# One tile per pair for the local exponentials, a mask added in three steps, and a new order of the plan

## The chip, the cores and the metric

The kernel runs on one core of a Trainium2 chip. The metric is the device time of one execution in microseconds (us). Before the change it is 983.41 us, the median of three runs (981.79 to 986.02). For this kernel about 0.5%, 4.9 us, can be told from no change.

The core has five engines with an instruction stream each: PE (TensorE, matmuls; PEld is its weight loads), DVE (VectorE), ACT (ScalarE), POOL (GpSimd) and SP (SyncE, which here only issues DMAs). They wait for each other and for DMAs through semaphores.

## The reference

Two attentions over q, k, v of shape 8 x 8 x 576 x 64 are added, and a feed-forward layer with a rational activation follows:

```python
q_d, k_d, v_d = (x.reshape(B, H, S // 4, 4, D).mean(axis=3) for x in (q, k, v))
out_up = np.repeat(sm_attn(q_d, k_d, v_d), 4, axis=2)        # attention among means of 4 tokens
mask = np.abs(pos[:, None] - pos[None, :]) < 4
scores = np.where(mask, scale * q @ k.T, -1e9)               # local attention, 7 tokens wide
out_local = softmax(scores) @ v
x = (out_up + out_local).transpose(0, 2, 1, 3).reshape(4608, 512)
h = x @ w_in                                                 # 512 -> 2048
P = a[0] + a[1] * h + a[2] * h**2 + a[3] * h**3
Q = 1 + abs(b[0]) * abs(h) + abs(b[1]) * h**2
out = (P / (Q + 1e-6)) @ w_out                               # 2048 -> 512
```

## The kernel before

**The layer.** The 4608 tokens are cut into blocks: eight of 512 tokens (one per batch) and a last one of the 64 tokens left of each batch. A block of 512 has 16 steps. In a step PE makes a 128 x 512 piece of h (line 1087, 12 matmuls), ACT and DVE make the activation from it (`middle`; ACT line 1100, DVE lines 1144 to 1193, each over 128 x 512), and PE multiplies the two parts of the result, `g`, into the output sums (line 1217, 12 matmuls). Line 1179 writes `g`; the first matmul of line 1217 waits for it.

**The attention.** Two heads make a pair, two pairs a quad, so a block has two quads. While PE works on the layer of one block, the attention of a later block is worked in between. From block 3 on (`begin`, called for ten quads, called far quads below) a quad goes like this. SP loads q and k. PE makes the local scores: 10 windows of 58 queries against 64 keys for each pair, two windows of one column of 64 to each head (line 484). DVE adds the mask while it moves the scores from PSUM to SBUF (line 498), takes the maximum (592), scales it (619); ACT takes the exponentials in place, 10 instructions a pair (627); DVE divides by the sums (668, 669, 692). These numbers then have to be turned. DVE turns 32 x 32 blocks (779, into `tt`), and SP sends them through DRAM to put the blocks in their places: four writes `bounce<-tt` and two reads `eu<-bounce` a pair (747). The pooled attention takes the same way (754, 757, `bounce_p`, `eq`). PE then multiplies with the values (929, 891).

**Where the tiles lie.** The scores, the exponentials (`el`) and what comes back from DRAM (`eu`) of a pair share one place in SBUF. The places of the two pairs of a quad (slots 0 and 1) lie side by side, and a tensor `els` is laid over both. All instructions on `el` of either pair go through views of `els` (lines 310 to 312), which lets one mask addition cover the last column of the first pair and all five columns of the second (line 519). `eu0` and `eu1` are tensors of their own at the same addresses (line 301).

**What sets the order.** Each piece of work is recorded as a task with the engine, an assumed duration, and the 32-byte pieces of SBUF or banks of PSUM that it reads and writes (`add`; `part` gives a view its own pieces). `Plan.run` then walks through time and puts the tasks of each engine in an order by their latest start; a table `SHIFT` moves that latest start, task by task. The instructions are issued in that order. It is the plan's own bookkeeping, by pieces, that decides the order; the semaphore waits are put in afterwards by the framework, by the tensors that instructions use.

```python
both = put("els", [P, NW, 2, D], F32, slots[0].el.at)
s.el = part(both, both.ap[:, i * NW // 2 : (i + 1) * NW // 2], i * n, n)
self.eu = put(f"eu{i}", [P, 4, NW // 2, BL], F32, self.el.at)
```

Of the kernel before, what the change touches and what calls it, by code (L numbers as in the profile page):

```python
# [20 lines left out]
P = 128  # L21
# [50 lines left out]
class Task:  # L72
    __slots__ = ("engine", "dur", "fn", "due", "preds", "succs", "late", "start", "end", "n", "load", "at", "key", "wait", "land", "big")


class Plan:
# [16 lines left out]
    def add(self, engine, dur, fn, reads=(), writes=(), due=None, load=None, at=0.0, wait=2.05, big=False):  # L93
# [3 lines left out]
        t.key, t.wait, t.big = self.key, wait, big  # L97
# [27 lines left out]
    def run(self):  # L125
# [10 lines left out]
        done, landed, served = [], [], 0.0  # L136
# [10 lines left out]
        while len(done) < len(self.tasks):  # L147
# [36 lines left out]
            if t.load is not None:  # L184
                t.land = max(at + t.wait, served) + t.load
                served = t.land
                if e == "SP":
                    landed.append(t.land)
                    if len(landed) >= self.RING:
                        free[e] = max(free[e], landed[-self.RING])  # L190
# [12 lines left out]
def attention_moe(  # L203
# [69 lines left out]
    maskd = put("maskd", [P, 2, NW // 2, D], BF16, maskb.at)  # L273
# [6 lines left out]
    class Slot:  # L280


        def __init__(self, i, at=None):
# [7 lines left out]
            if i % 2:  # L291
                self.el = one("el", [P, NW // 2, 2, D])
# [5 lines left out]
            if not i % 2:  # L298
                self.el = one("el", [P, NW // 2, 2, D])
# [8 lines left out]
    n = NW * D * 4  # L308
    assert slots[1].el.at == slots[0].el.at + n
# [6 lines left out]
    els = part(both, both.ap[:, split:], 8 * split * D, 8 * D * (NW // 2 + 1))  # L316
# [117 lines left out]
    def load_pooled(c, at=0.0):  # L434
# [5 lines left out]
        for dst, src, cost in ((s.pq, qkp, 0.4), (c.vp, None if c.far else vp, 0.25)):  # L440
            add("SP", ISSUE, lambda d=dst, x=src: nc.sync.dma_start(out=d.ap, in_=rows(x, 0)), (), (dst,), load=cost, at=at)
            for r in range(1, POOL):
# [5 lines left out]
                    (dst,), (dst,), load=1.8 * cost, wait=2.6,  # L448
# [42 lines left out]
    def scores_two(pair, bk, before=None, due=None):  # L491
# [20 lines left out]
        masked(4 * D, split, head, maskd.ap[:, 0, :split])  # L512
# [5 lines left out]
        add("PE", 1.06, rest, (s.qk, t.qk), bk, due=due[1])  # L518
        masked(0, NW // 2 + 1, els, flat(maskd.ap.rearrange("p i c k -> p (i c) k")).rearrange("p (c k) -> p c k", k=D)[:, split : split + NW // 2 + 1])
# [35 lines left out]
    def scores_pooled(cs, bk, due=None):  # L555
# [14 lines left out]
        add("PE", 1.095 if len(cs) == 2 else 0.6, issue, [c.slot.pq for c in cs], bk, due=due)  # L570

    def softmax_local(c, bk):
# [6 lines left out]
        if c.b >= MASK_LATE and not c.far:  # L579
# [5 lines left out]
                    in1=maskd.ap[:, 0].unsqueeze(1).broadcast_to([P, 2, NW // 2, D]),  # L585
# [292 lines left out]
    def weighted(cs, bk, due):  # L878
# [104 lines left out]
        if cs[0].far:  # L983
# [6 lines left out]
            def second(then=None, reads=()):  # L990
# [5 lines left out]
                add("PE", 0.82 if then is None else 1.29, issue, (*ready, *halves, *reads), avb, due=due)  # L996
# [4 lines left out]
            add("PE", 1.79, first, turn + pooled_v + ready + halves, ava, due=due - LEAD_A)  # L1001
# [279 lines left out]
    for r in range(POOL):  # L1281
        v = vf[r // 2]
        if r % 2:
            add(
                "POOL", 0.93, lambda r=r, v=v: nc.gpsimd.dma_start(out=v.ap, in_=vp[0, r], accum_op=ALU.add),
                (v,), (v,), load=3.0, wait=2.6,
            )
        else:
            add("SP", ISSUE, lambda r=r, v=v: nc.sync.dma_start(out=v.ap, in_=vp[0, r]), (), (v,), load=1.7)
# [18 lines left out]
    def attend(b):  # L1308

        last = due_h(blocks[b].first) - SPLIT_EARLY - 3.0  # L1310
        if b == MASK_LATE:
            mark("mask")
            for g in range(2):
                for i in range(2):
                    src = mask[:D, g, :].rearrange("p (c k) -> p c k", k=D)
                    add(
                        "SP", ISSUE,
                        lambda g=g, i=i, src=src: nc.sync.dma_start(out=maskd.ap[g * D : (g + 1) * D, i], in_=src),
                        (), (maskd,), load=0.2,
                    )  # L1320
        x, y = banks[0:2]

        def begin(b, q, before=None):
# [5 lines left out]
            mark("scores", q)  # L1329
# [111 lines left out]
    with tc.manual_schedule(engines={getattr(ET, e) for e in ("PE", "DVE", "Activation", "Pool", "SP")}):  # L1441
# [60 lines left out]
SHIFT = {  # L1502
# [4 lines left out]
    },  # L1507
# [4 lines left out]
    },  # L1512
# [4 lines left out]
    },  # L1517
# [4 lines left out]
    },  # L1522
    "h.0": {0: 62.6, 1: -31.1, 2: -30.3, 3: 307.1},
    "h.1": {0: 6.7, 1: -24.6, 2: -92.9, 3: -2.1},
# [207 lines left out]
```

## Time and profile before

| what | value |
|---|---|
| median of three runs | 983.41 us |
| the profiled execution's own time | 986.53 us |
| its span in the profile | 984.6 us |
| PE busy | 940.1 us, 95% |
| DVE busy | 874.2 us, 89% |
| ACT busy | 771.4 us, 78% |
| granted TensorE clock, mean | 0.987 |

The profile is of one execution. An engine is busy while an instruction of it runs; the time between is idle, and the profile says what ended each idle stretch (the releaser). PE's clock has two levels, 1.2 and 2.4 GHz; a granted clock of 0.50 over a stretch is the lower one. A busy PE is not always at full speed, so the clock has to be read beside the busy time.

### The profile page before, as it was taken

Reading aid. Unit: us, or ns where it says so; the run is one execution under the profiler, and the core shown is the slowest. Engines: PE = TensorE matmul, PEld = TensorE weight load, DVE = VectorE, ACT = ScalarE, POOL = GpSimd, SP = SyncE. Lnnn points to the kernel's source line nnn. Section 1 sums busy time; section 2 is a strip of 40 time slices with the busy share of each in tenths; the row PEclk is TensorE's granted clock in tenths of the full one; section 3 lists DMA queues with packets and bytes.
Section 4 is the critical chain, followed back from the end, with each engine's and each line's share of the span. In section 5 each row is a group of like instructions: output and inputs, shape, how many; then the busy total and the mean of one; then the engine's idle time right before and its main releaser. Section 6 shows DMA issues by size and latency. Waiting matters only on the chain.

```text
span 984.6 us, 19790 instructions
## 1 busy us (share of the span) xinstructions
PE 940.1 (95%) x7046; PEld 735.2 (75%) x7046; DVE 874.2 (89%) x1557; ACT 771.4 (78%) x1972; POOL 148.9 (15%) x176
## 2 busy tenths in 40 slices
PE   7999999799999999999999999989899999999997
PEld 6845556678777777877878787877787888888886
DVE  6789999799999888989899898989899988988886
ACT  3889999679788768886989688967798677777764
POOL 1031323111302121121303030404020000000000
PEclk9999999899999999999999999999999999999999
DMA  9487854536555555564566465646453000001001
GB/s 302 176 268 210 242 104 80 145 80 125 105 115 150 107 130 111 156 120 112 99 180 100 123 109 145 127 120 108 107 128 82 2 32 12 1 0 44 1 1 43
DMA packets 97738, 108.33 MB, mean 110 GB/s; under 512 B 29512, under 2 KB 79944, under 8 KB 97640
## 3 DMA queue, kind: packets, MB, share of 16 engines
q1 hardware_dynamic: 74120, 85.88, 29.3%
q0 software_dynamic: 23232, 20.66, 15.7%
q8 instruction: 56, 0.92, 0.4%
q10 hardware_dynamic: 288, 0.52, 0.2%
q14 instruction: 42, 0.34, 0.1%
HBM read 86.03 MB, written 20.99 MB: 109 GB/s over the span
## 4 chain that ended last, share of the span: by engine, by line
PE 46%; ACT 19%; DVE 17%; DMA 11%; issue 5%; SPq 1%; DVEq 0%; ACTq 0%
PE psum L1217 22%; PE psum L1087 20%; ACT m L1100 6%; ACT els L627 6%; DMA eu<-bounce 5%; ACT gb L1100 4%; DVE g L1179 4%; DVE m L1184 2%; DVE m L1149 2%; DMA sl<-in_w_out_dram 2%; DVE m L1144 1%; PE psum L891 1%; DMA st<-in_w_in_dram 1%; ACT ep L657 1%; DVE m L1193 1%
## 5 line engine op out<-in xcount | busy, mean ns | idle before, releaser
L1217 PE MATMUL psum<-wh,g 128*128 128x512 f32 x1152 | 378.2, 403 | 20.6 <-DVE g L1179 20.6
L1217 PEld LDWEIGHTS psum<-wh,g 128*128 128x128 f32 x1152 | 216.4, 190 | 80.7 <-DVE g L1179 27.2
L1087 PE MATMUL psum<-xs,wh 128*128 128x512 f32 (+1 forms) x1040 | 261.0, 389 | 2.5 <-ACT gb L1100 1.7
L1100 ACT ACTIVATE m<-psum,cf 128x512 f32<-128x512 f32 x288 | 207.3, 740 | 32.7 <-DVE m L1193 18.5
L1217 PE MATMUL psum<-wl,g 128*128 128x512 f32 x576 | 227.3, 395 | 0.0
L1087 PEld LDWEIGHTS psum<-xs,wh 128*128 128x128 f32 x1040 | 193.6, 189 | 45.1 <-ACT gb L1100 3.2
L1179 DVE TENSOR_TENSOR g<-m,m 128x512 fp32r<-128x512 f32 x288 | 194.9, 684 | 25.3 <-ACT m L1100 19.0
L1087 PE MATMUL psum<-xs,wl 128*128 128x512 f32 (+1 forms) x520 | 138.0, 387 | 0.0
L1100 ACT ACTIVATE gb<-m 128x512 f32<-128x512 f32 x144 | 92.4, 642 | 44.1 <-DVE m L1144 33.4
L1217 PEld LDWEIGHTS psum<-wl,g 128*128 128x128 f32 x576 | 109.9, 191 | 21.7
L1100 ACT ACTIVATE m<-psum 128x512 f32<-128x512 f32 x144 | 86.5, 600 | 47.1 <-PE psum L1087 36.3
L1144 DVE SCALAR_TENSOR_TENSOR m<-m,cf,m 128x512 f32<-128x512 f32 x144 | 107.5, 747 | 15.5 <-ACT m L1100 15.5
L1100 ACT ACTIVATE gb<-psum,cf 128x512 f32<-128x512 f32 x144 | 113.3, 787 | 10.0 <-PE psum L1217 9.8
L1087 PEld LDWEIGHTS psum<-xs,wl 128*128 128x128 f32 x520 | 96.4, 188 | 19.9
L1153 DVE TENSOR_TENSOR m<-m,gb 128x512 f32<-128x512 f32 x144 | 98.9, 687 | 13.9 <-ACT gb L1100 11.0
L445 POOL DMA_DIRECT2D pq<-in_qkp_dram x84 | 74.0, 929 | 196.1 <-DMA pq<-in_qkp_dram 135.2
L445 POOL DMA_DIRECT2D vq<-in_vq_dram x60 | 52.3, 910 | 329.5 <-DMA vq<-in_vq_dram 276.4
L1149 DVE TENSOR_TENSOR m<-m,m 128x512 f32<-128x512 f32 x144 | 98.5, 684 | 2.7 <-ACT m L1100 2.5
L1184 DVE SCALAR_TENSOR_TENSOR m<-m,g 128x512 f32<-128x512 f32 x144 | 98.8, 686 | 1.6
L1193 DVE TENSOR_TENSOR m<-m,m 128x512 f32<-128x512 f32 x144 | 98.9, 687 | 1.2
L1100 ACT ACTIVATE m<-gb 128x512 f32<-128x512 f32 x144 | 92.0, 639 | 3.6 <-DVE m L1149 1.9
L627 ACT ACTIVATE els<-els,nm 128x64 f32<-128x64 f32 x240 | 80.5, 347 | 18.0 <-DVE nm L619 9.4
(106 smaller groups left out, 894.8 us busy)
## 6 DMA issues: line engine op xcount, KB each, us to landing
qk<-in_qk_dram SPq DMA_DIRECT2D x32, 590.0 KB, 4.4
pq<-in_qkp_dram POOLq DMA_DIRECT2D x84, 144.0 KB, 3.7
vw<-in_vw_dram SPq DMA_DIRECT2D x32, 320.0 KB, 4.4
out_dram<-xf SPq DMA_DIRECT2D x34, 256.0 KB, 2.5
bounce<-tt SPq DMA_DIRECT2D x96, 80.0 KB, 2.0
eu<-bounce SPq DMA_DIRECT2D x40, 160.0 KB, 3.0
sl<-in_w_out_dram SPq DMA_DIRECT2D x12, 512.0 KB, 4.1
vq<-in_vq_dram POOLq DMA_DIRECT2D x60, 96.0 KB, 2.9
```

The costliest lines, as they stand in the source:

```text
L445: lambda d=dst, x=src, r=r: nc.gpsimd.dma_start(out=d.ap, in_=rows(x, r), accum_op=ALU.add),
L627: nc.scalar.activation(out=s.el.ap[:, k, j, :], in_=view[:, j, k, :], func=AF.Exp, bias=nm[:, 5 * j + k : 5 * j + k + 1], scale=scale, acc ...
L657: nc.scalar.activation(out=s.ep.ap[:, i, :], in_=view[:, i, :], func=AF.Exp, bias=nm[:, i : i + 1], scale=scale / 16.0, accum_out=sm[:, NW ...
L1087: nc.tensor.matmul(ph.ap[:, f * t : (f + 1) * t], lhsT=(high, low)[j][0][fc].ap[:, c, :], rhs=blk.x[i].ap[:, c, t0 : t0 + t], start=(part_ ...
L1100: add("ACT", cost, lambda: nc.scalar.activation(out=out_.ap, in_=in_, func=func, **kw), (room_in, cf, *more), (out_,))
L1144: lambda: v.scalar_tensor_tensor(out=tb.ap, in0=tq.ap, scalar=b1, in1=tb.ap, op0=ALU.mult, op1=ALU.add),
L1149: add("DVE", 0.602, lambda: v.tensor_tensor(out=ta.ap, in0=ta.ap, in1=tq.ap, op=ALU.mult), (ta, tq), (ta,))
L1153: add("DVE", 0.602, lambda: v.tensor_tensor(out=ta.ap, in0=ta.ap, in1=u.ap, op=ALU.add), (ta, u), (ta,))
L1179: return v.tensor_tensor(out=out, in0=x, in1=y, op=ALU.mult)
L1184: lambda: v.scalar_tensor_tensor(out=tb.ap, in0=tb.ap, scalar=CONE, in1=gh.ap.bitcast(F32), op0=ALU.add, op1=ALU.mult),
L1193: add("DVE", 0.602, lambda: v.tensor_tensor(out=ta.ap, in0=ta.ap, in1=tb.ap, op=op), (ta, tb), (ta,))
L1217: nc.tensor.matmul(ob[sub].ap, lhsT=g[i].ap[:, g0 : g0 + P], rhs=flat((high, low)[j][1][fc].ap), start=(fc == 0 and m == 0), stop=(fc == N ...
```

## The change

Four things are changed. The tensor `els` goes: `el0` and `el1` are tensors of their own. The mask addition of a far quad, two DVE instructions before (4 columns; then 6 columns of which one is the first pair's), becomes three (4 and 1 columns into `el0`, 5 into `el1`), and the mask is loaded once per partition and not twice, by two DMAs and not four. The plan's assumed durations are changed in a few places, and it now counts the second half of an accumulating DMA's traffic by itself (`more`, `owed`). The table `SHIFT` is another one, so that most instructions stand in another order on all engines. No other instruction is added or taken away, but for the plan's dummy matmuls at the start (line 1426), 166 before and 157 now.

```diff
-    maskd = put("maskd", [P, 2, NW // 2, D], BF16, maskb.at)
+    maskd = put("maskd", [P, NW // 2, D], BF16, maskb.at)
...
-            if i % 2:
-                self.el = one("el", [P, NW // 2, 2, D])
             self.qk = one("qk", [P, 2, SW])
...
-            if not i % 2:
-                self.el = one("el", [P, NW // 2, 2, D])
+            self.el = one("el", [P, NW // 2, 2, D])
...
-    both = put("els", [P, NW, 2, D], F32, slots[0].el.at)
-    for i, s in enumerate(slots):
-        s.el = part(both, both.ap[:, i * NW // 2 : (i + 1) * NW // 2], i * n, n)
...
-    els = part(both, both.ap[:, split:], 8 * split * D, 8 * D * (NW // 2 + 1))
...
-        masked(0, NW // 2 + 1, els, flat(maskd.ap.rearrange("p i c k -> p (i c) k")).rearrange("p (c k) -> p c k", k=D)[:, split : split + NW // 2 + 1])
+        masked(0, NW // 2 - split, part(s.el, s.el.ap[:, split:], 8 * split * D, 8 * (NW // 2 - split) * D), maskd.ap[:, split:])
+        masked(D, NW // 2, t.el, maskd.ap)
...
-                    (dst,), (dst,), load=1.8 * cost, wait=2.6,
+                    (dst,), (dst,), load=2.6 * cost, wait=2.6,
...
-            add("PE", 1.79, first, turn + pooled_v + ready + halves, ava, due=due - LEAD_A)
+            add("PE", 2.0, first, turn + pooled_v + ready + halves, ava, due=due - LEAD_A)
...
 SHIFT = {
-    "mask": {0: 57.4, 1: 106.3, 2: 66.3, 3: -1.4},
+    "mask": {1: 7.1},
...
```

The first place shown is DVE in the fourth far quad (the one of the chain below), around the division and the turning of the quad's later pair. `els` or `el0` are the exponentials, `sm` the sums, `tt` and `tp` the turned blocks, `g` and `m` the layer's tiles; what a row waits for stands behind it, `DMAHW` being the DMA queues' semaphores. Before:

```order
L668 TENSOR_SCALAR sm1_186<-sm1_186 128x13 [waits Activation_49]
L1153 TENSOR_TENSOR m1_162<-m1_162,gb1_172 128x512 [waits DVE_49,Activation_49]
L669 RECIPROCAL sm1_186<-sm1_186 128x13 [waits DVE_49]
L1179 TENSOR_TENSOR g2_169<-m0_161,m4_165 128x512 [waits PE_49]
L692 TENSOR_TENSOR els_213<-els_213,sm1_186 128x640 [waits DMAHW1_49,DVE_49]
L754 STREAM_TRANSPOSE tp1_212<-ep1_210 128x384 [waits Activation_49]
L757 STREAM_TRANSPOSE tp1_212<-ep1_210 128x96
L779 STREAM_TRANSPOSE tt1_205<-els_213 128x640 [waits DMAHW7_49,DVE_49]
L1179 TENSOR_TENSOR g1_168<-m1_162,m5_166 128x512 [waits PE_49,Activation_49]
```

And now, where line 689 is what 692 was, 776 what 779 was, 1176 what 1179 was:

```order
L665 TENSOR_SCALAR sm0_185<-sm0_185 128x13 [waits Activation_49]
L1176 TENSOR_TENSOR g2_169<-m0_161,m4_165 128x512 [waits DVE_49,PE_49]
L666 RECIPROCAL sm0_185<-sm0_185 128x13 [waits DVE_49]
L1141 SCALAR_TENSOR_TENSOR m3_164<-m5_166,cf_179,m3_164 128x512 [waits Activation_49]
L689 TENSOR_TENSOR el0_196<-el0_196,sm0_185 128x640 [waits DVE_49]
L1150 TENSOR_TENSOR m1_162<-m1_162,gb1_172 128x512 [waits Activation_49]
L776 STREAM_TRANSPOSE tt0_193<-el0_196 128x640 [waits DMAHW3_49,DMAHW2_49,DMAHW7_49,DMAHW1_49,DVE_49]
L751 STREAM_TRANSPOSE tp0_201<-ep0_199 128x384 [waits DMAHW3_49,DMAHW1_49,DMAHW4_49,DMAHW0_49,Activation_49]
```

The division no longer waits for any DMA; the layer's instructions stand at other places between, and pair 0 is now the later one. The DMAs that 776 and 751 wait for are those that last used the place of `tt0` and `tp0` (which is that of `qk0`).

The second place is SP's queue in the same quad, the earlier pair's way through DRAM. Before:

```order
L747 DMA bounce_p<-tp0_201 32x4x64 [waits DMAHW0_49]
L747 DMA eu0_198<-bounce 64x2x320 [waits DMAHW1_49,Activation_49]
L747 DMA bounce_p<-tp0_201 16x64 [waits DMAHW2_49]
L747 DMA eq0_200<-bounce_p 48x3x16 [waits DMAHW5_49,DMAHW4_49,DMAHW3_49]
L747 DMA eq0_200<-bounce_p 48x3x128 [waits DMAHW7_49,DMAHW6_49,DMAHW0_49]
L747 DMA eq0_200<-bounce_p 48x3x16
L747 DMA eq0_200<-bounce_p 48x3x128 [waits DMAHW2_49]
L747 DMA eu0_198<-bounce 64x2x320 [waits DVE_49]
L427 DMA qk0_191<-in_qk_dram 128x1180
```

And now:

```order
L744 DMA bounce<-tt1_204 32x4x160 [waits DMAHW7_49]
L744 DMA eq1_211<-bounce_p 48x3x16 [waits DMAHW1_49,DMAHW0_49,Activation_49]
L744 DMA eq1_211<-bounce_p 48x3x16 [waits DMAHW6_49,DMAHW2_49]
L744 DMA eq1_211<-bounce_p 48x3x128 [waits DMAHW4_49,DMAHW3_49]
L744 DMA eu1_209<-bounce 64x2x320 [waits DMAHW7_49]
L744 DMA eu1_209<-bounce 64x2x320
L744 DMA eq1_211<-bounce_p 48x3x128 [waits DMAHW5_49]
L423 DMA qk1_202<-in_qk_dram 128x1180
```

Before, the two reads into `eu0` waited for ACT and for DVE; now they wait for DMAs alone. In the new order the last `bounce` write and three reads of `eq` stand right ahead of them.

## Rows read from the trace of the kernel before

**Rows 1.** The page: busy time of each engine
```profile
PE 940.1 (95%) x7046; PEld 735.2 (75%) x7046; DVE 874.2 (89%) x1557; ACT 771.4 (78%) x1972; POOL 148.9 (15%) x176
```

**Rows 2.** Busy time in four stages: stage, length, engines, PE clock, DMA share, GB/s
```profile
0.00:48.31 48.31, 42.14 (x673) 34.49 (x673) 33.23 (x70) 29.87 (x109) 2.53 (x8) 0.96 0.71 239
48.31:182.25 133.94, 120.55 (x887) 74.04 (x884) 122.34 (x235) 119.85 (x344) 36.64 (x42) 0.98 0.69 180
182.25:753.37 571.12, 552.98 (x4391) 441.51 (x4392) 520.27 (x951) 464.19 (x1260) 109.69 (x126) 0.99 0.54 120
753.37:984.60 231.23, 224.39 (x1100) 185.14 (x1100) 198.33 (x304) 157.45 (x262) 0.00 (x0) 0.99 0.06 19
```

**Rows 3.** Waits: engine, what it waited for; us in total, times, longest
```profile
PE psum L1217 <- DVE g L1179: 20.6, 13, 4.6
...
PE psum L891 <- DMA eu<-bounce: 0.4, 1, 0.4
...
PE psum L929 <- DMA eq<-bounce_p: 0.2, 1, 0.2
```

**Rows 4.** Chain that ended last, 425 to 446 us: start, us, what
```profile
432.29 1.70 ACT m L1100 x3
433.99 4.20 DMA eu<-bounce
...
438.28 0.83 DVE els L692
...
439.13 2.88 DMA eu<-bounce
...
442.11 0.06 DVE tt L779
...
442.87 0.66 DVE g L1179
```

**Rows 5.** Instructions on tile els: engine idle before them until (us, times)
```profile
  DMA eu<-bounce: 27.8, 13
```

**Rows 6.** PE in order of time at four gaps: start, us, ... [idle before]
```profile
182.25 0.80 PE L1217 MATMUL psum<-wh,g 128*128 128x512 f32 x1 [4.56 <-DVE g L1179]
...
495.11 0.50 PE L1217 MATMUL psum<-wh,g 128*128 128x512 f32 x1 [0.41 <-DVE g L1179]
...
753.37 0.50 PE L1217 MATMUL psum<-wh,g 128*128 128x512 f32 x1 [0.85 <-DVE g L1179]
...
974.08 1.20 PE L1217 MATMUL psum<-wh,g 128*128 128x512 f32 x4 [0.30 <-DVE g L1179]
```

**Rows 7.** Stretches right behind four of PE's gaps, columns as in rows 2
```profile
182.25:187.31 5.06, 5.06 (x12) 4.00 (x13) 4.62 (x8) 2.87 (x6) 0.00 (x0) 0.50 0.57 144
...
338.05:341.70 3.65, 3.65 (x9) 2.95 (x10) 3.62 (x6) 1.72 (x4) 0.00 (x0) 0.54 0.38 78
...
443.58:446.90 3.32, 3.32 (x9) 2.66 (x10) 3.32 (x6) 1.39 (x3) 0.00 (x0) 0.59 0.35 72
...
650.10:653.50 3.40, 3.40 (x15) 2.79 (x16) 3.40 (x6) 1.47 (x3) 0.00 (x0) 1.00 0.32 67
```

**Rows 8.** Groups by line and shape, DVE's mask additions: busy us, mean ns
```profile
L498 DVE TENSOR_TENSOR els<-psum,maskd 128x768 f32<-128x768 f32 x10 | 9.5, 952 | 0.6 <-PE psum L484 0.6
...
L498 DVE TENSOR_TENSOR els<-psum,maskd 128x512 f32<-128x512 f32 x10 | 6.9, 686 | 0.0
...
L583 DVE TENSOR_TENSOR els<-psum,maskd 128x640 f32<-128x640 f32 x4 | 3.3, 821 | 0.0
```

**Rows 9.** Two far quads, from gap to gap, columns as in rows 2
```profile
443.58:495.11 51.53, 51.12 (x400) 40.84 (x400) 46.40 (x85) 40.09 (x112) 10.47 (x12) 0.97 0.52 105
495.11:546.02 50.91, 49.30 (x400) 39.57 (x400) 47.48 (x89) 43.69 (x117) 10.41 (x12) 1.00 0.64 147
```

**Rows 10.** A stretch of the second stage, columns as in rows 2
```profile
150.00:175.00 25.00, 24.74 (x182) 15.56 (x180) 24.70 (x47) 24.74 (x85) 7.78 (x10) 1.00 0.48 92
```

**Rows 11.** DMA issues: what, count, KB each, median us to landing
```profile
eu<-bounce SPq DMA_DIRECT2D x40, 160.0 KB, 3.0
```

More of the change, by code (lines that the diff above doesn't have):

```diff
@@ L72 @@
 class Task:
-    __slots__ = ("engine", "dur", "fn", "due", "preds", "succs", "late", "start", "end", "n", "load", "at", "key", "wait", "land", "big")
+    __slots__ = ("engine", "dur", "fn", "due", "preds", "succs", "late", "start", "end", "n", "load", "at", "key", "wait", "land", "big", "more")
 class Plan:
@@ L91, in mark, with add @@
         self.key = ".".join(str(x) for x in name), 0
-    def add(self, engine, dur, fn, reads=(), writes=(), due=None, load=None, at=0.0, wait=2.05, big=False):
+    def add(self, engine, dur, fn, reads=(), writes=(), due=None, load=None, at=0.0, wait=2.05, big=False, more=None):
         t = Task()
@@ L96, in add @@
         t.preds, t.succs, t.late, t.start = {}, [], 1e9, None
-        t.key, t.wait, t.big = self.key, wait, big
+        t.key, t.wait, t.big, t.more = self.key, wait, big, more
         self.key = t.key[0], t.key[1] + 1
@@ L135, in run @@
         free = dict.fromkeys(self.ENGINES, 0.7)
-        done, landed, served = [], [], 0.0
+        done, landed, owed, served = [], [], [], 0.0
         def release(t):
@@ L184, in run @@
             if t.load is not None:
-                t.land = max(at + t.wait, served) + t.load
-                served = t.land
+                if e == "SP" and len(owed) > 2:
+                    served += owed.pop(0)
+                t.land = max(at + t.wait, served if t.more != 0.0 else 0.0) + t.load
+                if t.more != 0.0:
+                    served = t.land
                 if e == "SP":
+                    if owed or t.more:
+                        owed.append(t.more or 0.0)
                     landed.append(t.land)
@@ L511, in scores_two @@
             before(lambda: scores_far(pair[0], range(split), bk, 4 * D), (s.qk,))
-        masked(4 * D, split, head, maskd.ap[:, 0, :split])
+        masked(4 * D, split, head, maskd.ap[:, :split])
         def rest():
@@ L568, in issue @@
                         )
-        add("PE", 1.095 if len(cs) == 2 else 0.6, issue, [c.slot.pq for c in cs], bk, due=due)
+        add("PE", 1.13 if len(cs) == 2 else 0.6, issue, [c.slot.pq for c in cs], bk, due=due)
     def softmax_local(c, bk):
@@ L994, in issue @@
                         then()
-                add("PE", 0.82 if then is None else 1.29, issue, (*ready, *halves, *reads), avb, due=due)
+                add("PE", 0.84 if then is None else 1.31, issue, (*ready, *halves, *reads), avb, due=due)
                 for c, x in zip(cs, avb):
@@ L1285, in attention_moe @@
                 "POOL", 0.93, lambda r=r, v=v: nc.gpsimd.dma_start(out=v.ap, in_=vp[0, r], accum_op=ALU.add),
-                (v,), (v,), load=3.0, wait=2.6,
+                (v,), (v,), load=2.1, wait=6.4, more=0.0,
             )
         else:
-            add("SP", ISSUE, lambda r=r, v=v: nc.sync.dma_start(out=v.ap, in_=vp[0, r]), (), (v,), load=1.7)
+            add("SP", ISSUE, lambda r=r, v=v: nc.sync.dma_start(out=v.ap, in_=vp[0, r]), (), (v,), load=1.7, more=2.1)
     for c in c0:
@@ L1313, in attend @@
             for g in range(2):
[L1314 to L1320, printed above, removed]
+                src = mask[:D, g, :].rearrange("p (c k) -> p c k", k=D)
+                add(
+                    "SP", ISSUE,
+                    lambda g=g, src=src: nc.sync.dma_start(out=maskd.ap[g * D : (g + 1) * D], in_=src),
+                    (), (maskd,), load=0.3,
+                )
         x, y = banks[0:2]
@@ L1328, in begin @@
                 load_qk(c), load_pooled(c)
-            mark("scores", q)
+            mark("scores" if before else "alone", q)
             scores_two(pair, [x, y], before, [end - lead for lead in FAR[:2]])
@@ L1531 @@
+    "h.1": {0: -24.4, 3: -2.6},
+    "h.2": {1: 46.5, 2: 67.8, 3: 19.6},
+    "h.3": {0: -14.9, 1: -7.7, 2: 16.4, 3: 50},
+    "h.4": {0: 465.8, 1: 36.8, 2: -116.2, 3: 112.2},
+    "h.5": {0: 217.5, 1: -27.9, 2: 279.9},
+    "h.6": {2: 173.8},
+    "h.7": {0: 38.4, 1: 7.7, 2: -2.1},
     "load": {
-        0: -17.4, 1: 17.7, 3: -17.9, 4: 8.3, 5: -2.2, 6: 0.7, 7: -87.8, 8: -0.2, 9: 5.9, 10: -5, 11: 7.4,
-        12: -17.4, 13: -26.9,
+        0: -109.3, 1: -1.8, 2: 1.2, 4: 24.9, 5: -47.2, 6: 18.7, 7: -38.8, 8: 9, 9: -30.9, 10: 1.4,
+        11: -16.5, 12: 23.6, 13: 18.5,
@@ L1632 @@
-    "scores.1": {0: 26.4, 1: -14.3, 2: 16.6, 3: -14.4, 4: -2.7, 6: 26.6, 7: 18.6},
-    "setup": {0: -1.3, 2: 14.7, 3: 17.2, 4: 7.8},
[6 rows of a table removed]
[8 rows of a table added]
+    },
+    "scores.0": {0: 97.5, 1: 5.8, 2: 3.2, 3: 119.5, 4: -10.9, 5: -54.1, 6: 76.1, 7: 8.2, 8: -0.5},
+    "scores.1": {0: 58.2, 1: -20.6, 2: 1.1, 3: 48.5, 4: 44, 5: -2.7, 6: 34.3, 7: 58.1, 8: 20.3},
+    "setup": {0: -53.4, 1: 13.4, 2: -22.5, 3: 99.9, 4: -14.3},
[6 rows of a table added]
     "turned.0": {
[4 rows of a table removed]
[4 rows of a table added]
     },
     "turned.1": {
[4 rows of a table removed]
-    },
[10 rows of a table removed]
[4 rows of a table added]
+    },
[10 rows of a table added]
 }
```

65 lines of the change are left out of this document (26 added, 39 removed), and 153 rows, old and new, of the table SHIFT.

## The prediction

> **What bounds the kernel now.** I read the busy times first, then the stages, PE's waits, the chain behind one of them, and last what stands on the tile that the change cuts in two.
>
> PE is busy for 940.1 us of a span of 984.6 [rows 1], so 44.5 us of idle time is all that a better order could give back on PE, and more only where its clock is low. By stage [rows 2]: 6.2 us of it lie in the first 48 us, 13.4 us from 48 to 182 us, 18.1 us from 182 to 753 us, where the far quads run, and 6.8 us behind them. In the second stage ACT and DVE are the full ones: from 150 to 175 us they are busy for 24.74 and 24.70 of 25 us [rows 10]. In the third stage PE is: a far quad takes 50.91 us and holds 49.30 us of PE work at the full clock, and 47.48 us of DVE work [rows 9].
>
> PE's longest wait is for `g` from DVE's line 1179: 20.6 us in 13 places [rows 3]. One is 0.30 us at 974 us, behind all attention [rows 6]. The other 12, together 20.3 us, stand at 182 us and at the end of the far quads. What made DVE late there is to be seen in the chain at 443 us [rows 4]. ACT comes to the end of its exponentials and the ops behind them; a read `eu<-bounce` starts at 433.99 us and takes 4.20 us; only then does DVE divide (line 692, 0.83 us); a second `eu<-bounce` takes 2.88 us; only then does DVE turn the blocks (779); then comes `g`, 0.66 us, and PE goes on. The reads belong to one pair and the division and the turning to the other. Nothing in the computation ties them together. They are tied because both pairs' exponentials are views of `els`, over which `eu0` and `eu1` lie. The plan's bookkeeping is by 32-byte pieces and does not know this tie, so it orders DVE's work as if there were no wait. In all, engines sat idle before work on `els` for 27.8 us, 13 times, until an `eu<-bounce` had landed [rows 5].
>
> **The false waits go.** In the order the division waits for a DMA before and not now, and the two reads into `eu` wait for ACT and DVE before and for DMAs alone now. So the wait for the other pair's reads can't come back; the 20.3 us of PE's idle time lose their cause. What is late next is PE itself, with 49.30 us of work in a quad against 47.48 of DVE. I don't take all of it: the plan's assumed durations are not the chip's, and some gap will stay where a quad ends. The two far quads with the smallest single gaps show 0.41 and 0.85 us [rows 6]; their mean, 0.63 us, left in each of the 12 places keeps 7.6 us. Gain: 20.3 - 7.6 = **12.7 us**. The bounds are 0 (each gap finds another cause) and 20.3.
>
> **The low clock behind the gaps.** After three of the gaps PE runs at a low clock for some microseconds [rows 7]: 5.06 us at a granted 0.50, 3.65 at 0.54, 3.32 at 0.59, where 1.2 GHz is 0.50. Against the full clock that costs 5.06 x 0.50 + 3.65 x 0.46 + 3.32 x 0.41 = 2.5 + 1.7 + 1.4 = 5.6 us. A gap of the same kind before 650.10 us left the clock at 1.00, so it doesn't follow every gap; with gaps of 0.6 us I expect it after none. Gain: **5.6 us**, bounds 0 and 5.6.
>
> **The third mask addition.** Ten far quads have one DVE instruction more. The trace has 512 elements at 686 ns, 768 at 952 and 640 at 821 [rows 8]: 266 ns for 256 elements, 1.04 ns each. One column of both heads is 128 elements, 686 - 384 x 1.04 = 287 ns. The new pair costs 287 + 821 - 952 = 156 ns more, 1.6 us over ten quads. It lies under PE: DVE has 49.30 - 47.48 = 1.8 us to spare in a quad. Cost: **0**; 1.6 us if that cover is gone. The first pair's maximum has to wait for the added instruction, but neither pair waits for the other's scores now. The two mask DMAs less are issued once, beside other loads: 0.
>
> The Trainium skill, "VectorE: DVE Perf Modes", section "Rules for kernel authors", speaks against this edit: for chained DVE work one should keep the number of operations low and not mind the semaphores. By that rule the change would cost the 1.6 us and give nothing for the waits. The trace agrees on the fixed cost of an operation (the 156 ns above), but the waits here are for transfers through DRAM that hold DVE for microseconds, and those the rule does not weigh. It is the fourth case below.
>
> **The new order elsewhere.** The table moves nearly every instruction and no row can price that. In the second stage ACT and DVE leave no room, so an order can only move the 8.8 us that PE idles there beside the gap at 182 us (13.4 - 4.56 [rows 2, 6]): from 8.8 us less to as much more. I take 0, since the work of ACT and DVE is the same and they are full. The last stage is PE's own work at the full clock, and the dummy matmuls at the start only fill time in which PE waits: 0.
>
> **Sum.** 12.7 + 5.6 = 18.3 us off the profiled execution's 986.53 us makes 968.2 us. That execution lies 3.1 us over the median of 983.41, so I forecast 968.2 - 3.1 = **965 us**.
>
> **The rivals.**
>
> - *More comes back.* All 20.3 us go, the clock holds, and the second stage loses its 8.8 us too: 34.7 us, 949 us. For it: the rows price each piece. Against it: it asks the plan to be right everywhere. Anything under 955 us counts here. Chance 0.13.
> - *Another wait takes the place.* DVE still has 47.48 us to do in a far quad, in bursts where attention and layer meet, and ACT's exponentials are where they were. If the ends of the quads are late for that reason, only the gap at 182 us goes, where DVE sat for the whole of a read: 4.56 - 0.63 + 2.5 of clock = 6.4 us, less 1.6 for the mask: 978.6 us. For it: some chains end in ACT's exponentials. Against it: in the chain of rows 4 DVE stands still, it is not busy. Chance 0.13, a third of it under 978.5 us.
> - *SP's queue becomes the wait; slower.* In the new order `eu` is read behind a `bounce` write and `eq` reads that each wait for earlier transfers, and whatever is behind them on SP waits too. If PE came to its value matmuls (929, 891) before `eu` had landed, each of the ten far quads would pay up to one landing, 3.0 us [rows 11], and as much as 1.9 us of low clock (5.6 / 3): up to 49 us, 1,014 us; my guess in this case is 1,000. It decides from (988.3 - 965) / 10 = 2.3 us a quad. Against it: before, PE waited 0.4 us for `eu` and 0.2 for `eq`, once each [rows 3], although these reads were held back by ACT and DVE. Chance 0.06.
> - *Only the number of operations counts, or the waits return under another name.* No wait is worth anything, the mask costs 1.6 us: 985 us. Against it: the waits of DVE's division in the two orders. Chance 0.05.
>
> **How the numbers follow.** The forecast, 955 to 978 us, has the rest, 0.63. Faster by over 0.5% (under 978.5 us; 0.5% is what a measurement of this kernel can tell from no change): 0.63 + 0.13 + 0.04 = 0.80. Within 0.5%: 0.09 + 0.05 = 0.14. Slower: 0.06. The range is 950 to 981 us: below, nearly the case in which all comes back; above, the case of another wait; what it leaves out is the slower case, the fourth one and a little of the first.
>
> **What would show it.** Right: no engine idle on `el` until an `eu<-bounce`; PE's wait for line 1179's `g` at about 8 us and not 20.6; the granted clock at 1.00 throughout the third stage; far quads of about 50 us. The third mask addition shows as ten instructions of about 0.29 us with PE busy beside them. The second stage should keep its idle time but for the gap at 182 us. Wrong: PE waiting for `g` in as many places with DVE busy in them (the second rival), PE waiting for `eu` or `eq` (the third), or a second stage that is longer or shorter by more than 5 us, in which case the table and not the tile did it.

## The result, and the profile after

The changed kernel takes **952.59 us** (median of 4 runs, 949.43 to 954.72), against 982.60 us for the kernel before on the same chip (4 runs, 979.13 to 986.02): a ratio of 0.9692, 95% interval 0.9647 to 0.9737. I forecast 965, in a range of 950 to 981. The sign is right and the time lies in the range, but 12 us that the sum did not hold have come off as well.

The profiled execution took 953.53 us, with a span of 951.5. Its busy line, which answers to [rows 1]:

```profile
PE 931.4 (98%) x7037; PEld 731.9 (77%) x7037; DVE 874.3 (92%) x1567; ACT 775.4 (81%) x1972; POOL 149.2 (16%) x176
```

PE's idle time fell from 44.5 us to 951.5 - 931.4 = 20.1, by 24.4; PE's busy time fell by 940.1 - 931.4 = 8.7, of which the nine dummy matmuls less are some 1 us (166 were busy for 14.0 us, 157 for 12.9) and the rest, with nothing else taken away, goes to the clock, whose mean rose from 0.987 to 0.997. Together that is the 33.1 us by which the span is shorter. The forecast had 12.7 of idle time and 5.6 of clock.

Over the stretches of [rows 2], the last one cut at the new end:

```profile
0.00:48.31 48.31, 45.26 (x672) 34.77 (x673) 37.57 (x79) 33.23 (x115) 2.52 (x8) 1.00 0.81 273
48.31:182.25 133.94, 131.88 (x981) 86.29 (x980) 133.46 (x253) 132.58 (x369) 37.22 (x42) 1.00 0.71 185
182.25:753.37 571.12, 564.47 (x4506) 454.86 (x4505) 538.74 (x985) 475.01 (x1270) 109.50 (x126) 1.00 0.53 117
753.37:951.50 198.13, 189.74 (x882) 156.03 (x881) 164.51 (x253) 134.60 (x220) 0.00 (x0) 0.99 0.05 17
```

The third stage gave what was expected of it: PE's idle time went from 18.1 us to 6.7. But the first stage's went from 6.2 to 3.1 and the second's from 13.4 to 2.1. Of these 14.4 us only 4.56 are the gap at 182 us. In the second stage ACT did 119.85 us of work in 133.94 before and 132.58 now, DVE 122.34 and 133.46: neither was full before.

PE's waits, which answer to [rows 3]:

```profile
PE psum L926 <- DMA eq<-bounce_p: 5.4, 4, 2.9
PE psum L1214 <- DVE g L1176: 2.2, 4, 1.2
PE psum L527 <- ACT el L624: 1.8, 1, 1.8
```

The wait for `g` has fallen from 20.6 us to 2.2, and the two longest of the four that are left (1.17 and 0.64 us) stand at 942 and 945 us, behind all attention. A new one has come: PE waits for `eq` four times in the far quads, where it waited 0.2 us once. The longest is at 491 us. The chain ahead of it:

```profile
481.76 2.46 DMA bounce_p<-tp
...
484.25 0.35 SPq L744
...
484.65 0.43 SPq L423
...
485.12 0.42 SPq L744
...
485.59 5.15 DMA eq<-bounce_p
...
491.09 1.42 PE psum L926 x20
```

Between two reads of `eq` SP issues line 423, the 590 KB load of the next `qk`; the read behind it takes 5.15 us. Behind this gap the clock is low, as in [rows 7], once in the whole third stage:

```profile
491.09:494.50 3.41, 3.41 (x73) 3.25 (x74) 0.22 (x2) 0.49 (x4) 0.00 (x0) 0.60 0.12 31
```

The mask additions, which answer to [rows 8]:

```profile
L494 DVE TENSOR_TENSOR el<-psum,maskd 128x640 f32<-128x640 f32 x10 | 8.2, 817 | 0.0
L494 DVE TENSOR_TENSOR el<-psum,maskd 128x512 f32<-128x512 f32 x10 | 6.8, 680 | 0.0
...
L494 DVE TENSOR_TENSOR el<-psum,maskd 128x128 f32<-128x128 f32 x10 | 2.8, 280 | 0.0
```

280 + 817 - 952 = 145 ns more a quad; I had 156.

And the first stage, which the prediction did not look into. What ACT waited for from 16 to 180 us, before:

```profile
ACT sl L375 <- DMA sl<-in_w_in_dram: 4.0, 3, 2.3
ACT cf L355 <- DMA cf<-in_coef_dram: 3.3, 1, 3.3
ACT sm L375 <- DMA sm<-in_w_in_dram: 2.4, 1, 2.4
ACT sl L375 <- DMA sl<-in_w_out_dram: 1.4, 2, 0.7
```

and after:

```profile
ACT sl L371 <- DMA sl<-in_w_in_dram: 1.7, 2, 1.0
...
ACT sl L371 <- DMA sl<-in_w_out_dram: 0.3, 1, 0.3
```

11.1 us before, 2.0 after. Only the wait for `cf` lies in the first stage; the other 7.8 us lie in the second, where ACT's longest single wait is another, the one that ends at 182 us:

```profile
ACT m L1100 <- DVE g L1179: 5.7, 1, 5.7
```

The plainest of ACT's waits for DMAs is the absolute value of two coefficients, `cf`. In ACT's order of time, before:

```profile
18.12 0.68 ACT L375 ACTIVATE st<-st 128x512 f32<-128x512 f32 x1 [0.23 <-DMA st<-in_w_out_dram]
22.13 0.20 ACT L355 ACTIVATE cf<-cf 128x2 f32<-128x2 f32 x1 [3.33 <-DMA cf<-in_coef_dram]
22.24 0.30 ACT L627 ACTIVATE el<-psum,nm 128x64 f32<-128x64 f32 x1
...
23.68 0.28 ACT L733 COPY et<-psum 128x128 f32<-128x128 f32 x1
```

ACT stands for 3.33 us before an instruction of 0.20 us. Ten exponentials and the copy of `et` are behind it, and PE waits for that copy (3.31 us, at 24.02 us). After, the same instruction stands at 26.62 us, its DMA has landed, and neither ACT nor PE waits there:

```profile
26.62 0.21 ACT L351 ACTIVATE cf<-cf 128x2 f32<-128x2 f32 x1
```

### The profile page after: what moved, and what is told of

It is laid out like the page before. It is cut to its first block, busy times and chain, and to the rows that moved or that the text cites. A ratio compares the mean times of both kernels' runs of the same rounds, so it can differ in the third digit from the quotient of the medians.

```text
span 951.5 us, 19814 instructions
## 1 busy us (share of the span) xinstructions
PE 931.4 (98%) x7037; PEld 731.9 (77%) x7037; DVE 874.3 (92%) x1567; ACT 775.4 (81%) x1972; POOL 149.2 (16%) x176
## 3 DMA queue, kind: packets, MB, share of 16 engines
q0 software_dynamic: 23232, 20.66, 16.2%
## 4 chain that ended last, share of the span: by engine, by line
PE 47%; DVE 26%; ACT 16%; issue 5%; DMA 3%; SPq 2%; DVEq 0%; ACTq 0%
PE psum L1214 19%; PE psum L1084 17%; ACT m L1097 7%; DVE g L1176 6%; PE psum L1072 4%; DVE m L1181 3%; DVE m L1190 3%; DVE m L1141 3%; DVE m L1146 3%; ACT gb L1097 3%; ACT el L624 2%; PE psum L888 2%; DMA eq<-bounce_p 2%; DVE m L1150 2%; SPq L744 1%
## 5 line engine op out<-in xcount | busy, mean ns | idle before, releaser
L1214 PE MATMUL psum<-wh,g 128*128 128x512 f32 x1152 | 373.1, 398 | 3.2 <-DVE g L1176 2.2
L1084 PE MATMUL psum<-xs,wh 128*128 128x512 f32 (+1 forms) x1040 | 258.1, 388 | 0.8 <-ACT gb L1097 0.8
L1097 ACT ACTIVATE m<-psum,cf 128x512 f32<-128x512 f32 x288 | 213.2, 748 | 26.4 <-PE psum L1084 20.3
L1214 PE MATMUL psum<-wl,g 128*128 128x512 f32 x576 | 224.5, 391 | 0.0
L1097 ACT ACTIVATE gb<-psum,cf 128x512 f32<-128x512 f32 x144 | 115.4, 802 | 21.2 <-PE psum L1214 20.7
L624 ACT ACTIVATE el<-el,nm 128x64 f32<-128x64 f32 x240 | 80.8, 355 | 1.7 <-DVE nm L616 1.7
```

Source lines behind the costliest of these rows:

```text
L624: nc.scalar.activation(out=s.el.ap[:, k, j, :], in_=view[:, j, k, :], func=AF.Exp, bias=nm[:, 5 * j + k : 5 * j + k + 1], scale=scale, acc ...
L1084: nc.tensor.matmul(ph.ap[:, f * t : (f + 1) * t], lhsT=(high, low)[j][0][fc].ap[:, c, :], rhs=blk.x[i].ap[:, c, t0 : t0 + t], start=(part_ ...
L1097: add("ACT", cost, lambda: nc.scalar.activation(out=out_.ap, in_=in_, func=func, **kw), (room_in, cf, *more), (out_,))
L1214: nc.tensor.matmul(ob[sub].ap, lhsT=g[i].ap[:, g0 : g0 + P], rhs=flat((high, low)[j][1][fc].ap), start=(fc == 0 and m == 0), stop=(fc == N ...
```

## The experiments

Theory: the tile takes away the false waits and gives what the sum held (some 18 us); the table gives the rest, ahead of the far quads, where ACT no longer stands behind late DMAs. Rivals: the table alone does it all; the tile without the table gives nothing lasting; the first stage is paced by the weights' transfers, whatever ACT's order. PE's idle time, as length less busy time of two windows, is the thread through them; the median stands beside it.

| kernel | median, us | ratio to before, 95% | PE idle, first 200 us | PE idle, behind |
|---|---|---|---|---|
| before | 982.6 | | 19.6 | 25.0 |
| changed | 952.6 | 0.9692 (0.9647, 0.9737) | 5.1 | 15.0 |
| tile alone | 961.9 | 0.9764 (0.9726, 0.9801) | 16.2 | 12.5 |
| order alone | 967.2 | 0.9822 (0.9798, 0.9846) | 7.1 | 21.8 |
| tile, new order of the first stage | 956.0 | 0.9735 (0.9711, 0.9759) | 10.3 | 11.8 |
| tile, new order of two stages | 953.7 | 0.9715 (0.9692, 0.9739) | 8.4 | 13.8 |
| changed, qk behind eq | 949.3 | 0.9653 (0.9627, 0.9679) | 7.3 | 10.8 |

Lines of the code shift by a few in each; the operations are the same. The runs were made on several chips, whose own runs of the kernel before have medians from 980.9 to 983.7 us, so a difference of 2 or 3 us between two medians of this table can be the chip's; the ratios are each to the runs of before on the same chip, and differ by up to 0.0014 from the quotients of the medians.

**The tile alone.** The kernel before with every instruction in its old order, but tensors of their own for the two pairs:

```diff
-    both = put("els", [P, NW, 2, D], F32, slots[0].el.at)
-    for i, s in enumerate(slots):
-        s.el = part(both, both.ap[:, i * NW // 2 : (i + 1) * NW // 2], i * n, n)
...
+        def both():
+            added(0, NW // 2 - split, tail, maskd.ap[:, 0, split:])
+            added(D, NW // 2, t.el, maskd.ap[:, 0])
```

> The kernel before in its own order on every engine, but el0 and el1 are tensors of their own (so the second mask addition is two instructions, 1 and 5 columns, issued as one task of the plan with the old assumed duration). Theory of the tile: the ties between the two pairs go, and with them PE's waits for g behind reads of eu and the low clock after them; the first 175 us keep their idle time. The changed kernel lost 21.5 us less than before in its first 200 us, 7.1 of which are the gap at 182 us with its clock, so I expect 19 us less than before (7.1 there and about 12 in the far quads): 963 us, from 958 to 968. Rival, the order did it: 980 to 985 us, DVE idle for other reasons in the same places.

Measured: 961.86 us (957.84 to 965.31). PE's waits:

```profile
PE psum L937 <- DMA eq<-bounce_p: 5.1, 4, 2.0
PE psum L899 <- ACT et L741: 3.6, 1, 3.6
...
PE psum L899 <- DMA eu<-bounce: 1.2, 2, 0.8
...
PE psum L1225 <- DVE g L1187: 0.3, 1, 0.3
```

In the old order the wait for `g` is gone but for the one at the end: the false waits were its cause, in all 12 places. Waits for `eq` and `eu` have come up in their stead, 6.3 us where there were 0.6. (At 540 us, for one, the late read of `eq` was issued right behind a load of `qk` and took 4.04 us.) The gap for `et` near 24 us stands as before.

**The order alone.** The changed kernel in its exact order, with the two pairs' exponentials again views of one tensor:

```diff
-            self.el = one("el", [P, NW // 2, 2, D])
...
+    both = put("els", [P, NW, 2, D], F32, slots[0].el.at)
+    for i, s in enumerate(slots):
+        s.el = part(both, both.ap[:, i * NW // 2 : (i + 1) * NW // 2], i * n, n)
```

> The changed kernel in its own order on every engine, its three mask additions kept, but el0 and el1 are views of one tensor laid over both, as before the change. Theory of the tile, effects that add up: the first stage keeps its gain of about 14 us, the waits for the other pair's eu come back: 982.6 - 14 = 969 us, from 965 to 975. Theory of an interaction (the new order is packed on the assumption that there are no ties, so a tie costs it more than it cost the old order): 978 us or more. Rival, the order did it all: 951 to 957 us.

Measured: 967.15 us (963.76 to 968.79). PE's first wait, and what held the engines idle before work on `els`, the second of which answers to [rows 5]:

```profile
PE psum L1222 <- DVE g L1184: 10.3, 13, 2.0
```

```profile
  DMA eu<-bounce: 14.7, 9
```

The tie is back and DVE stands behind the reads again, for half as long as in the old order. Most of what the order gives alone lies in the first 200 us (19.6 to 7.1 us of idle time, 3.2 us behind). The two kernels' gains, some 21.9 and 16.6 us against the runs of before beside them, add to 8.5 us more than the change's 30.0: the gap at 182 us, 4.56 us and 2.5 of clock behind it, is gone in both.

**Forty more mask additions.** The changed kernel, where each addition of five columns is five of one:

```diff
-            add(
-                "DVE", 0.08 + 2 * n * D / 960,
-                lambda: nc.vector.tensor_tensor(
...
+            def issue():
+                for k in range(n) if n == NW // 2 else (slice(None),):
...
+            add("DVE", 0.08 + 2 * n * D / 960, issue, (*bk, maskd), (out,))
```

> The changed kernel in its own order, but each addition of the mask over five columns is five instructions of one column: 40 DVE instructions more, at 0.287 us for one column against 0.821 for five (5 x 0.287 - 0.821 = 0.61 us a far quad, 6.1 us over ten). Theory of the prediction (this work lies under PE, DVE has about 1.8 us to spare in a far quad): within 1.5 us of the changed kernel, 951 to 955 us. Rival, DVE is now the bound in the far quads: 6 us more, 958 to 960 us.

Measured: 954.68 us (953.75 to 957.19), ratio 0.9704 (0.9686 to 0.9722).

```profile
L497 DVE TENSOR_TENSOR el<-psum,maskd 128x128 f32<-128x128 f32 x60 | 12.8, 279 | 0.0
```

By their durations forty more should take 50 x 279 - 10 x 817 ns = 5.8 us. But instructions back to back overlap: these 60 additions are busy for 12.8 us and not for 60 x 279 ns = 16.7 us, where they were for 8.2 + 2.8, and DVE in all for 876.3, where it was for 874.3. The time rose by 2.1 us, and the intervals overlap. So the rival's 958 to 960 was not met and the theory's 951 to 955 was, but how much of it PE hides is not shown, since DVE had only 2.0 us more to do. By the medians forty more cost some 2 us, which is not clear of the noise; ten would then cost half a microsecond.

**One ACT instruction moved, in the old order.** The tile alone, with the operation on `cf` just ahead of its first reader:

```diff
+    todo.remove(coef_task[0])
+    todo.insert(next(i for i, t in enumerate(todo) if t.key[0].startswith("middle")), coef_task[0])
```

> The order of before and a tile for each pair (961.9 us in the run above), with one ACT instruction moved: the absolute value of the coefficients (cf) stands just ahead of its first reader and not ahead of the first pooled exponentials. Theory: part of what the new order gave in the first 200 us came from ACT no longer standing behind a late DMA; then ACT's wait for cf (3.7 us in the window 16 to 180 us) and PE's gap at 24 us (3.6 us) go, and the time is 958 to 959 us. Rival: the weight DMAs set the pace of the first stage, ACT then waits as much longer for a weight tile, and the time stays at 961 to 962 us.

Measured: 959.37 us (954.69 to 960.94), ratio 0.9747 (0.9719 to 0.9775). ACT's longest waits from 16 to 180 us:

```profile
ACT sl L371 <- DMA sl<-in_w_in_dram: 3.5, 2, 2.0
ACT sm L371 <- DMA sm<-in_w_in_dram: 2.8, 2, 2.3
ACT sl L371 <- DMA sl<-in_w_out_dram: 1.3, 2, 0.7
```

The wait for `cf` is gone, ACT waits hardly longer for the weights in its stead (7.6 us; 7.1 without the move), and PE's wait for `et` has fallen from 3.6 us to 0.4. PE's idle time in the first 200 us fell from 16.2 to 12.8 us. The time is 0.4 us above the theory's 958 to 959.

**The same instruction put back, in the new order.** The changed kernel with the operation on `cf` ahead of the first pooled exponentials:

```diff
+    todo.remove(coef_task[0])
+    todo.insert(next(i for i, t in enumerate(todo) if t.engine == "ACT" and t.key[0] == "first.1" and t.dur == 1.07), coef_task[0])
```

> The changed kernel with the same single ACT instruction put back to where it stood before the change, ahead of the first pooled exponentials. Theory (ACT behind a late DMA): ACT waits some 3 us for cf again, PE shows a gap of about 3 us near 24 us, and the time is 955.5 to 957 us. Rival (the first stage has another pace-maker in the new order): 952 to 953 us.

Measured: 955.85 us (952.36 to 957.50), ratio 0.9714 (0.9687 to 0.9741). ACT, and then PE, in order of time:

```profile
22.06 0.20 ACT L351 ACTIVATE cf<-cf 128x2 f32<-128x2 f32 x1 [3.66 <-DMA cf<-in_coef_dram]
```

```profile
25.04 1.22 PE L890 MATMUL psum<-et,vw 64*64 64x58 f32 x18 [3.34 <-ACT et L732]
```

Taken away in one order and put back in the other, the same instruction makes and unmakes the same gap. Its worth in time is 2.5 and 3.3 us by the medians, 1.7 and 2.2 by the ratios; that is near what was expected, though the intervals overlap those of the kernels without the move. The gap is shown; its worth of some 2 to 3 us rests on both agreeing.

**The weights' operations moved too.** ACT scales each weight tile that a DMA brings (line 375 of before). In the old order with the tile and the move of `cf`, each such operation stands up to four ACT instructions later, but ahead of its first reader:

```diff
+    for w in [t for t in todo if t.engine == "ACT" and t.dur == 0.565]:
+        here, first = todo.index(w), min(todo.index(x) for x in w.succs)
+        acts = [x for x in todo[here + 1 : first] if x.engine == "ACT"]
+        if acts:
+            todo.remove(w)
+            todo.insert(todo.index(acts[:4][-1]) + 1, w)
```

> The order of before, a tile for each pair and the coefficients' operation moved, as in the run of 959.4 us; now each of ACT's operations on a weight tile (which waits for the weight's DMA) stands up to four ACT instructions later too, as far as its first reader on DVE allows. Theory (an in-order ACT stands behind late weight DMAs, 7.6 us of such waits left there): ACT's waits for sl and sm fall to 2 to 4 us and the time to 955 to 957 us. Rival (the weights themselves are what the first stage waits for, so DVE and PE then wait for them): 958.5 to 961 us.

Measured: 961.89 us (958.27 to 964.02), ratio 0.9775 (0.9747 to 0.9803). ACT no longer has a weight DMA among its waits of over 0.9 us. DVE's waits from 16 to 180 us:

```profile
DVE wb L374 <- ACT st L371: 4.1, 5, 1.6
DVE wb L374 <- ACT sl L371: 1.5, 3, 0.8
...
DVE wb L374 <- ACT sm L371: 0.7, 1, 0.7
```

My theory fell here. The time is 0.9 us above the rival's range, and the trace shows the rival's wait: DVE splits these tiles at once and now waits 6.3 us for ACT to scale them, where it waited 2.4 us. The waits for `cf` and for the weights look alike in the trace. One stood before work that nothing else delayed; the others stood before work that is wanted next.

The same move in the changed kernel (with the load of `qk` moved as below):

> The changed kernel with the load of q and k behind the reads of eq (949.3 us), and ACT's weight operations moved up to four ACT instructions later. Only 3 us of ACT's waits for weights were left there, so the theory of the run just above gives at most 1 to 2 us, 947.5 to 949.5 us; the rival 949 to 951 us, or more if DVE now waits for the weights.

Measured: 955.97 us (955.31 to 956.19), ratio 0.9724 (0.9700 to 0.9747), against 0.9653 (0.9627 to 0.9679) without it: slower, by some 7 us, and the intervals are apart. DVE waits for the scaled tiles here too:

```profile
DVE wb L374 <- ACT sl L371: 4.6, 7, 1.1
DVE wb L374 <- ACT sm L371: 1.7, 3, 1.0
```

**The new order, only as far as the layer begins.** The tile alone, with the first 203 pieces of work in the changed kernel's order, and its 157 dummy matmuls in their places:

```diff
     todo = plan.run()
+    chosen = [plan.tasks[n] for n in TAKEN]
+    rest = set(chosen)
+    todo = chosen + [t for t in todo if t not in rest]
```

> The order of before with a tile for each pair (961.9 us), but its first 203 pieces of work, to the layer's first matmuls at about 45 us, stand in the changed kernel's order. In the first 50 us the kernel before loses 7.7 us of PE (6.2 idle, 1.5 of low clock) and the changed one 3.0. Theory that what is lost in the first stage is won there and nothing more: 957 us (956 to 958.5). Rival that an earlier start of the weights also empties the second stage: 951 to 955 us. Rival that the old order behind it takes the start back, since ACT and DVE have the same work: 960 to 962 us.

Measured: 956.01 us (953.33 to 957.63). **And as far as the far quads,** with 992 pieces:

> The order of before with a tile for each pair (961.9 us), but the first 992 pieces of work, to about 185 us, stand in the changed kernel's order; the far quads and the last stage keep the order of before. Theory that all the worth of the new order lies ahead of the far quads: the tile's kernel lost 16.9 us of PE in the first 180 us and the changed kernel 5.1, so 961.9 - 11.8 = 950 us (949 to 952). Rival that the new order is worth something in the far quads too: 953 to 956 us.

Measured: 953.67 us (952.77 to 954.71). By the medians, the new order of the first stage brings 5.9 of the 9.3 us between the tile alone and the whole change, that of the second another 2.3, and 1.1 are left for all behind. By the ratios (0.9764, 0.9735, 0.9715, 0.9692) each of the three steps is some 2 to 3 us and the whole 7, and neighbouring intervals overlap, so the times don't settle the split. The traces, one execution each, are plainer: PE's idle time in the first 200 us falls at each step, from 16.2 to 10.3, 8.4 and 5.1 us, and behind them it doesn't fall (12.5, 11.8, 13.8, 15.0). So what the order gives on top of the tile lies ahead of the far quads, as far as idle time shows it.

The first forecast is met. The second is missed by 1.7 us and falls in its rival's range, but the trace does not bear that rival out: behind 200 us this kernel idles for 13.8 us and the changed one for 15.0. It loses in two other places, in PE's waits:

```profile
PE psum L548 <- DVE el L591: 2.0, 1, 2.0
PE psum L571 <- DVE el L591: 1.8, 1, 1.8
```

The second, at 202 us, is close behind the place where the two orders are joined. The first, at 146 us, comes from this kernel having four loads of the mask where the changed one has two: the last two are issued at 140.6 us (the changed kernel's two at 106.5 and 107.8), and DVE waits for them.

```profile
145.39 0.82 DVE L591 TENSOR_TENSOR el<-psum,maskd 128x640 f32<-128x640 f32 x1 [1.91 <-DMA maskd<-in_mask_dram]
```

Less the 2.0 us that PE stands for it, the run would be at about 951.7 us by this estimate, inside its theory's range.

**The load of `qk` behind the reads of `eq`.** The changed kernel, with one kind of instruction moved on SP:

```diff
+    sp = [t for t in todo if t.engine == "SP"]
+    for n, t in enumerate(sp):
+        if t.key[0].startswith("load.") and t.load == 1.46:
+            eq = [x for x in sp[n + 1 : n + 5] if x.dur == 0.78 and x.wait == BACK]
+            if eq:
+                todo.remove(t)
+                todo.insert(todo.index(eq[-1]) + 1, t)
```

> The changed kernel with one thing moved on SP: the 590 KB load of the next q and k, which in each far quad stands among the reads of eq, is issued behind them. Theory: PE's new wait for eq (5.4 us, 4 times) comes from the reads sharing the DMA engines with that load; the wait falls to about 2 us and the time to 949 to 951 us. Rival: eq is late because of what SP waits for ahead of it, or q and k become late in turn; 952 to 954 us.

Measured: 949.31 us (948.05 to 951.61), the fastest kernel here. In the list of DMA issues, a 72 KB read of `eq` took, in the changed kernel:

```profile
eq<-bounce_p SPq DMA_DIRECT2D x40, 72.0 KB, 4.4
```

and with the load moved, where PE's wait follows in a second fence:

```profile
eq<-bounce_p SPq DMA_DIRECT2D x40, 72.0 KB, 2.2
```

```profile
PE psum L926 <- DMA eq<-bounce_p: 0.4, 1, 0.4
```

The median landing is halved, the wait falls from 5.4 us to 0.4, and no wait of PE for `qk` has come. That is shown; the time is less clear, as the intervals of the two ratios overlap, and it rests on the next run (0.9654) agreeing. The gain of 3.3 us is a little short of these 5.0; in the profiled execution the first 200 us idle 2.2 us more (7.3 against 5.1). With the stores of the output moved later too:

```diff
+        if t.key[0].startswith("store."):
+            eq = [x for x in sp[n + 1 : n + 9] if x.dur == 0.78 and x.wait == BACK]
```

> The kernel of the run just above with the stores of the output moved behind the reads of eq as well, where they stood within the eight SP instructions ahead of them. Theory (eq is read late because SP's instructions ahead of it wait): another 1 to 2 us less than the run above, 948 to 950 us, with no PE wait for eq over 0.5 us. Rival (only shared DMA engines matter): the same as the run above within 0.7 us.

Measured: 949.74 us (948.33 to 950.97): no change. The edit did less than was meant: most stores now stand between the reads and not behind them all. And only 0.4 us of PE's wait for `eq` was left to be won (0.3 now). So the run shows that stores ahead of the first reads cost nothing here, and not more.

## Why the prediction was right, and where it was not

- **The false waits (12.7 us of the sum): right.** The sum priced the tile, and the tile alone came out at 961.9 us where the sum had 965. With the tile alone in the old order PE's wait for `g` fell to 0.3 us. I kept back 7.6 us for gaps that would stay, and 5.7 did (5.1 + 1.2 us for `eq` and `eu`, less the 0.6 of before), so the term was 14.6 in that kernel and 20.3 - 5.2 = 15.1 in the changed one. A far quad takes 50.2 us, from the gap at 290.16 us to that at 491.09 four quads on; I had about 50. The reason I gave was wrong, though: it was not a plan that misjudged the end of a quad, but, as the run with `qk` moved shows for the changed kernel, reads of `eq` that follow a large load. That is the third rival's wait, at some 1.4 us in each of four quads, below its point of 2.3 us in each of ten.
- **The low clock (5.6 us): right in kind, small in size.** In the third stage the low stretches of [rows 7] are gone and one of 3.41 us at 0.60 has come, 1.4 us: 4.2 of the 5.6. But PE's busy time fell by 8.7 in all. Some 1 us of that is the dummy matmuls; most of the rest is the clock behind two gaps of before that the sum did not count, at 24 and at 68 us, 1.7 us each:

```profile
24.02:28.00 3.98, 3.98 (x57) 3.87 (x58) 1.28 (x4) 3.98 (x24) 0.00 (x0) 0.57 1.03 407
68.41:72.00 3.59, 3.59 (x50) 2.99 (x50) 3.38 (x7) 3.59 (x7) 2.13 (x4) 0.54 0.61 102
```

- **The third mask addition (0): right as far as the runs can tell.** 145 ns each, and forty more cost some 2 us by the medians, not clear of the noise. The Trainium skill, "VectorE: DVE Perf Modes", section "Rules for kernel authors", says that for chained DVE operations their number counts and not the semaphores. The tile alone has ten DVE operations more and is 2.4% faster; what it no longer waits for are DMAs, so taking that rule as a price for this edit, as the fourth rival did, would have been wrong here.
- **The new order elsewhere (0): the step that failed.** It was worth 7 us (by the ratios) to 9.3 us (by the medians) with the tile in place. I wrote that ACT and DVE leave no room in the second stage because they were full from 150 to 175 us [rows 10]. That slice is not the stage. The view by stages had ACT at 119.85 of 133.94 us, 14 us idle [rows 2], and another slice of before shows it:

```profile
100.00:125.00 25.00, 22.60 (x240) 13.68 (x239) 23.14 (x45) 22.72 (x73) 7.68 (x9) 1.00 0.82 220
```

  The same 25 us after:

```profile
100.00:125.00 25.00, 25.00 (x149) 15.37 (x148) 24.98 (x52) 24.61 (x86) 6.39 (x7) 1.00 0.72 208
```

  An engine that is idle for 14 us in a stretch that its neighbour PE waits in is an engine that waits. Its list of waits, one view away, named what for: of the 14 us, 5.7 are the wait at 182 us, which the sum had, and 7.8 are waits for three kinds of weight loads, which it had not. PE idles there for 8.8 us beside that gap, nearly all of it in waits for ACT. The first stage I had left out altogether. There the move of `cf` alone takes PE's idle time in the first 48 us from 6.3 to 3.4 us, where the changed kernel has 3.1, and is worth some 2 to 3 us. What makes up the second stage was not isolated. That the weights' operations merely stood too early is not borne out: moved later, they gained nothing. That their DMAs are issued earlier fits: the twelfth of the weight loads starts at 37.07 us and not at 44.54, and the DMA engines are busy for 0.81 of the first 48 us and not 0.71. But it is not the whole: with the new order of the first stage alone that load starts at 37.31 us, ACT still waits 5.3 us for weights (7.1 in the tile alone), and the second stage still idles for 7.4 us (9.1 in the tile alone, 2.1 in the changed kernel).
- **The check that I had set** was a second stage longer or shorter by more than 5 us, "in which case the table and not the tile did it". Its idle time fell by 11.3, 6.8 beyond the gap. The runs say both: about 22 us from the tile, 7 to 9 from the table on top.
- **The rivals.** The case in which more comes back, under 955 us, is what happened; I gave it 0.13. So the time lies in the range because the range was made wide enough for this rival; the forecast's own 955 to 978 us missed it. The rival's price for the second stage was right (8.8 us, of which 6.8 went). That its total of 949 us came so near is partly luck: it had neither the first stage nor the clock behind the gaps at 24 and 68 us, and not the 5.4 us that the new wait for `eq` took back. Another wait of `g` in the old one's place, and the number of operations as all that counts, are ruled out by the tile alone.

## What to carry to other kernels

Where waits are put in by the tensors that instructions use, a tensor laid over two buffers ties work on either to transfers into the other; look for an engine that idles before one buffer until a transfer into the other has landed. Read "full" from the whole stretch in which a cost is said to be hidden, and for an engine that isn't full read its own waits, and take off those that the sum has already, before giving a new order a zero. An instruction that waits for a late DMA and isn't wanted soon belongs behind whatever is ready; those whose results were wanted at once gained nothing from being moved, and in the changed kernel lost 7 us.

## What was not expected of the hardware

A DMA of 3 KB, issued among the first loads, took 16.4 us to land; what made it so late was not tried. Reads of 72 KB took 4.4 us (median of 40) with loads of 590 KB issued among them and 2.2 with these moved behind: how long they took was set by what was issued around them. In the changed kernel a gap of 2.88 us at 491 us was followed by 3.41 us at 0.60 of the clock, near the lower level, and one of 1.46 us at 290 us by a clock of 1.00 over the next 3.84 us. The first gap thus cost another 1.4 us behind it. The length of a gap alone doesn't decide this: in the kernel before, one of 1.87 us was followed by 0.54 at 338 us and one of 2.60 us by 1.00 at 650 us [rows 7].
